# Two transfers for each late load, two subtractions written in pairs and two more zero products in an induced-set attention and mixture-of-experts kernel

## The chip, the cores and the metric

The kernel runs on one core of one Trainium2 chip. The metric is the time of one execution in device microseconds (us); lower is better. Every number below comes from three timed executions of the kernel before and from one more execution that was taken with the hardware profiler.

## What is computed

Four batches of 11456 rows of 128 numbers go through two attentions over 32 inducing points, and the result, seen as 45824 rows, through a soft mixture of experts (8 experts with 4 slots each, inner width 1024). The softmax over rows (`d`) runs down all 45824 rows, so no output can be finished before the last row has been read.

```python
def mab(q, kv):
    s = scale * (q @ kv.transpose(0, 2, 1))
    s = s - s.max(-1, keepdims=True)
    a = np.exp(s)
    a /= a.sum(-1, keepdims=True) + 1e-09
    return a @ kv
h = mab(I, x)
x = mab(x, h).reshape(B * S, D)
...
logits = x @ phi
d = np.exp(logits - logits.max(0, keepdims=True))
d /= d.sum(0, keepdims=True) + 1e-09
slot_input = d.T @ x
slot_out[e] = np.maximum(slot_input[e] @ w1[e], 0.0) @ w2[e]
...
c = np.exp(logits - logits.max(1, keepdims=True))
c /= c.sum(1, keepdims=True) + 1e-09
return c @ slot_out
```

All of it is in fp32.

## The kernel before

The rows are cut into 24 tiles, 6 for each batch; a tile n has 15 blocks of 128 rows, 1920 columns and 960 KB. A tile is read as rows (`xn`, n) and transposed (`xt`, n); for n from 6 on both lie ready in memory and are two loads, `ldn` (line 282) and `ldt` (line 294), each one transfer of 128 rows of 7680 bytes. The weights follow as nine loads `w` (lines 741 and 743). All loads, and later all stores of results (line 1020), are issued by SyncE (SP) in one fixed order. Each transfer carries one of eight completion semaphores in turn, and the issue of a transfer waits until the one that used its semaphore before, eight transfers earlier, has landed; some also wait until an engine has let go of the buffer.

Four stages follow each other, and overlap:

- First attention (L329 `s1p`, L340, L386, L389, L405 `ha`): scores of the inducing points against a tile, exponentials, and `ha`, 15 small products on a tile that add up over the six tiles of a batch. When the last tile of a batch is in, a short chain (hs, L461; htp, L464; hts, L467) gives the keys of the second attention.
- Second attention (L329 `s2p`, L576 and L579 on VectorE, then L583 on GpSimd, exponentials on ScalarE, L592 and L605 on TensorE, L635 on GpSimd): the logits of a tile go into `l_all`.
- Dispatch, by segments of three tiles: the maximum of the segment (`t`/`tm`, `pt`, `mc`, `pb`, `m_all`), then for each tile d = logits - maximum (L706, on GpSimd for 19 tiles and on VectorE for tiles 12, 20, 21, 22, 23), its exponential (L709) and the products `u` (L719). After the last segment `wl` (L814, GpSimd), `us_all` (L826 GpSimd, L842 VectorE) and `sit` (L845 to L852, TensorE) join the segments, VectorE copies them into `ma` (L863), and the experts run on TensorE: `hpm` (L872), `htm` (L885), `so` (L901), then `sos` and `sr` (L908, L911) give the slot outputs `srs`.
- Output: the softmax over slots of each tile (lines 511 to 547, 967, 970), four products `po` with `srs` (L1000), four copies out of PSUM (L1011, shared by ScalarE and VectorE) and the stores. Until `srs` is there no store can start.

A *fill* is a product of a zeroed 128x128 tile with itself into a free PSUM buffer (line 235, `warm_into`): nothing reads it. The kernel has ten: one early, one and six around tile 17 of the dispatch, and two before the experts.

The order of the work on every engine is written out by hand: `plan.order()` reads a string of numbers (`ORDER`), and each engine runs its operations in that order, strictly one after the other. What stands later on an engine waits, even if its own inputs are there.

Where a subtraction L706 writes its tile, `DW` lists the tiles that are written block after block: of each pair of blocks the 32 numbers of the one, then of the other, so that the write steps while the read runs straight. Tiles that are not listed are written as they are read, the two blocks of a pair interleaved, and `u` reads them with a step of two.

Of the kernel before, what the change touches and what calls it, by code (L numbers as in the profile page):

```python
# [26 lines left out]
WP = XW  # L27
NW = 2 * E * F // WP
# [5 lines left out]
HOST_T = [6, 7, 8, 9, 10, 11, 12, 13, 14, 15, 16, 17, 18, 19, 20, 21, 22, 23]  # L34
# [15 lines left out]
RINGS = {'x': 13, 's1': 6, 'e1': 2, 's2': 9, 'a2t': 2, 'd': 3, 'half': 1, 'cs': 3, 'mm': 8, 'h': 1, 'hts': 2, 'ht': 1, 'bdg': 2, 'hc': 4, 'bm': 6, 'bz': 8, 'cm': 6, 'cz': 6, 'tms': 2, 'xa': 1, 'xb': 1, 'xc': 1, 'xd': 1, 'xe': 1, 'xf': 1}  # L50
H = 1
HEAD = 1
NF = 10
ORDER = (
# [7 lines left out]
    "8h8u9Id2667H8t7J9J837L7O7MaNaz9B9K9C9W7P8g9L9Xaaabdi7K7N7Qb19Y9MaAaOaBb2aPb3btbubvbwbxbybzbAbCaCac9Z9NaDada0aQaRa1b4aEaFb5aeaf9O8va29P9R8waSb6a38xag9QaT8y8za49SahaGaiaHb7a6akaIbDaJ"  # L62
    "aUa5aj8A8D8Galb88BaV7RaK8EamaWaMb9baaXanao8HaYbbb0bE8C8Fi28Iapasbc8JbFbei3i4i5i6i7i8bfaqatavawbGbgar9DbhaubIbJbHbi9EbKaxbLbMbjbObmbpbkbnaLbdaZbPbBbqbQaybSbNbYbZdud3bRblbobrbVbTbUbW"
    "d4c0dcdDbXi9iac3c4dLd5dUe3dddjdndvdkebc5c7c8c9c1c6dodpdwdqcadrdldxdEcdcbceccdycfcgdzdFc2ekdAdGchdsdBdtesdHdIdCcicjfCfFfDfEfGfHfwdMdJfJfLdKfIdNfKfNfMfOfPgDdVdWfxfAfyfzfQdOdPgGgFgEgH"
    "e4dXfWfUdQfRfTfSdRg3e5g0fYfXg7dYdZfZg6g4dSdTece6e7edeeg5eBe0eJgxe8gzgygBefg9gagceggbgde1gAe2e9elgfeheReaeteiglgnejghgigjgmemeueveCgKgpggeneoeDgNewexepgMgrgOgsgugLgogvgWeqeygteZereE"
    "gXgQezeKeLeFgReAgYeGgTeMgSgUgZeNeOh0eHfBgIfVgJg2g1g8gegkgCgqgPh2h5heh6h3h4h1h7gVgweIf7ePeSf0hgh8hieTffeQeUf1hfhaf2f3eVf8hqfohbf4eWhshteXeYf5fgf9faf6fphuh9hrhhhchkhlfbfchCfhhmfdfihD"
    "hFfjfqhGhwfrfshyfefthEhvhjhdhAhzfkflhxfuhnfvhHhIhMhohJhKfmfnhLhOhVhZhNhWhPhShXhQhYhRi0hUhphBhT"
# [28 lines left out]
def tag_of(kind, a):  # L96
    return (XTAG if kind == "xt" else NTAG).get(a, "x")
# [51 lines left out]
def tile_kernel(ctx, tc, x0, xn, xt_d, ind_t, phi, w12, w3, consts, out):  # L149
    nc = tc.nc  # L150
# [121 lines left out]
    def load(a):  # L272
# [388 lines left out]
    def segment(k):  # L661
# [72 lines left out]
    def weights():  # L734
        for o in range(0, 2 * E * F, WP):
            m = min(WP, 2 * E * F - o)

            def ld(o=o, m=m):
                t = btile("x", ("w", o // WP))
                if m == WP:  # L740
                    nc.sync.dma_start(parts(t), w12[o // WP].rearrange("h p w -> p h w"))
                else:
                    nc.sync.dma_start(t[:, :m], w3)
                wt.append(t)

# [392 lines left out]
```

## Time and profile before

| what | value |
|---|---|
| median of 3 executions | 216.58 us (216.47 to 217.27) |
| the profiled execution | 217.6 us, of it 215.5 us span from the first to the last instruction |
| TensorE | busy 188.7 us (88%) |
| VectorE | busy 162.6 us (75%) |
| ScalarE | busy 135.5 us (63%) |
| GpSimd | busy 125.5 us (58%) |
| data moved | 73.87 MB, mean 343 GB/s |
| mean granted TensorE clock | 0.915 of full speed |

The page of the profile divides the span into 40 slices. By it TensorE is busy almost throughout, but a busy share is a mean over stages that wait for different things. The loads fill the transfer engines until about 126 us, the transfers then rest until about 155 us, and the stores fill them to the end. The granted clock is full until 140 us and falls to half in one slice there and again in parts of the last 45 us. To see what one stage waits for, read the order of time on one engine, with the idle time before an instruction and what ended it.

### The profile page before, as it was taken

How to read it: one execution, taken by the hardware profiler on the slowest of the kernel's cores; microseconds unless marked ns; L12 is line 12 of the kernel's file. 1: busy time of each engine (PE TensorE's matmuls, PEld its weight loads, DVE VectorE, ACT ScalarE, POOL GpSimd, SP SyncE). 2: the span in 40 equal slices, each digit the busy share in tenths (PEclk: the TensorE clock that was granted, in tenths of full speed). 3: DMA queues.
4: the chain of work that ended last, by engine and by line, in shares of the span. 5: the costliest groups of instructions: out<-in, count | busy, mean ns of one | idle time of the engine just before them, and what ended most of it. 6: DMA issues, size and time to landing. Idle time of an engine off the chain costs nothing.

```text
span 215.5 us, 6873 instructions
## 1 busy us (share of the span) xinstructions
PE 188.7 (88%) x2778; PEld 129.7 (60%) x2778; DVE 162.6 (75%) x375; ACT 135.5 (63%) x368; POOL 125.5 (58%) x138
## 2 busy tenths in 40 slices
PE   7699999999999999999798999899799998998100
PEld 7368574598465986559694688798454375342000
DVE  0114576999999999999598999995999789855400
ACT  2487541965856993269683988604599898963300
POOL 0000000549988489987876999996857867742000
PEclk9999999999999999999999999969999958755855
DMA  6999999998799999999999950000299999999994
GB/s 218 387 429 416 393 422 415 415 415 361 233 389 422 422 412 419 408 419 412 415 416 414 419 236 0 6 5 3 66 378 410 418 421 422 412 421 423 411 416 190
DMA packets 12799, 73.87 MB, mean 343 GB/s; under 512 B 1633, under 2 KB 2657, under 8 KB 12769
## 3 DMA queue, kind: packets, MB, share of 16 engines
q1 hardware_dynamic: 12336, 73.27, 84.1%
q8 instruction: 22, 0.36, 0.7%
q10 hardware_dynamic: 432, 0.17, 0.3%
q14 instruction: 9, 0.07, 0.1%
HBM read 49.84 MB, written 23.59 MB: 341 GB/s over the span
## 4 chain that ended last, share of the span: by engine, by line
PE 59%; DMA 10%; DVE 9%; POOL 7%; issue 4%; ACT 3%; SPq 1%; DVEq 0%; ACTq 0%; POOLq 0%
PE po L1000 10%; PE s1p L329 9%; PE ha L405 9%; PE s2p L329 7%; DMA w<-w 6%; PE lp L605 6%; DMA xn<-xn 4%; DVE ot L1011 4%; PE tt L592 4%; PE tp L306 3%; POOL d L706 3%; PE hpm L872 2%; POOL bt L583 2%; PE u L719 2%; DVE l_all L970 2%
## 5 line engine op out<-in xcount | busy, mean ns | idle before, releaser
L1000 PE MATMUL po<-l_all,srs 32*128 32x480 f32 (+1 forms) x200 | 43.6, 746 | 3.8 <-DVE l_all L970 1.8
L1000 PEld LDWEIGHTS po<-l_all,srs 32*128 32x128 f32 x200 | 22.0, 229 | 24.4 <-ACT ot L1011 10.5
L1011 ACT COPY ot<-po 128x480 f32<-128x480 f32 (+1 forms) x65 | 31.8, 576 | 7.4 <-PE po L1000 7.1
L583 POOL TENSOR_TENSOR bt<-bt,bm 128x480 f32<-128x480 f32 x24 | 23.6, 1001 | 16.6 <-DVE bm L579 14.1
L967 POOL TENSOR_TENSOR ct<-ct,cz 128x480 f32<-128x480 f32 x24 | 23.7, 996 | 9.2 <-DVE cz L547 9.2
L605 PE MATMUL lp<-bdg,a2t 128*128 128x132 f32 x192 | 25.7, 278 | 0.6 <-ACT d L709 0.6
L340 DVE TENSOR_SCALAR_CACHE_REDUCE s<-s1p 128x480 f32<-128x480 f32 (+1 forms) x24 | 15.0, 644 | 14.2 <-PE s1p L329 13.8
L635 POOL TENSOR_TENSOR bt<-bt,bz 128x480 f32<-128x480 f32 x24 | 23.5, 1003 | 2.8 <-DVE bz L617 1.9
L605 PEld LDWEIGHTS lp<-bdg,a2t 128*128 128x128 f32 x192 | 23.3, 190 | 1.8 <-ACT d L709 0.8
L1011 DVE COPY ot<-po 128x480 f32<-128x480 f32 (+1 forms) x35 | 20.2, 602 | 3.3 <-PE po L1000 3.3
L706 POOL TENSOR_TENSOR d<-l_all,m_all 128x512 f32<-128x512 f32 x19 | 21.8, 1173 | 1.3 <-ACT m_all L685 1.3
L520 POOL TENSOR_TENSOR ct<-l_all,cm 128x512 f32<-128x512 f32 x18 | 18.8, 1053 | 3.9 <-DVE l_all L970 2.4
L405 PE MATMUL ha<-xn,e 128*32 128x128 f32 x570 | 19.6, 275 | 1.6 <-issue 1.5
L329 PE MATMUL s1p<-xt,it_sb 128*32 128x480 f32 x160 | 19.8, 571 | 0.8 <-ACT xt L314 0.7
L386 ACT ACTIVATE s<-s,negm 128x480 f32<-128x480 f32 (+1 forms) x24 | 16.6, 697 | 5.7 <-DVE negm L371 5.7
L329 PE MATMUL s2p<-xt,hts 128*32 128x480 f32 x160 | 19.6, 571 | 0.0
L405 PEld LDWEIGHTS ha<-xn,e 128*32 128x32 f32 x570 | 16.5, 109 | 4.1 <-issue 2.2
L709 ACT ACTIVATE d<-d 128x512 f32<-128x512 f32 x24 | 14.9, 633 | 5.9 <-POOL d L706 5.0
L342 POOL MEMSET s<- 128x16 f32 x4 | 0.5, 117 | 31.1 <-DVE e L389 30.8
L970 DVE STREAM_TRANSPOSE l_all<-ct 128x480 f32<-128x480 f32 x24 | 15.8, 660 | 1.9 <-POOL ct L967 1.9
L389 DVE STREAM_TRANSPOSE e<-s 128x480 f32<-128x480 f32 x24 | 15.6, 657 | 1.9 <-ACT s L386 1.7
L576 DVE STREAM_TRANSPOSE bt<-s2p 128x480 f32<-128x480 f32 x24 | 15.6, 665 | 0.8 <-PE s2p L329 0.4
(136 smaller groups left out, 369.5 us busy)
## 6 DMA issues: line engine op xcount, KB each, us to landing
out<-ot SPq DMA_DIRECT2D x20, 960.0 KB, 8.0
xn<-xn SPq DMA_DIRECT2D x18, 960.0 KB, 13.1
xt<-xt SPq DMA_DIRECT2D x14, 960.0 KB, 13.9
w<-w SPq DMA_DIRECT2D x8, 960.0 KB, 14.4
l_all<-xn SPq DMA_DIRECT2D x5, 960.0 KB, 10.0
l_all<-xt SPq DMA_DIRECT2D x4, 960.0 KB, 6.4
out<-ot SPq DMA_DIRECT2D x6, 480.0 KB, 6.7
xn<-x SPq DMA_DIRECT2D x2, 256.0 KB, 3.3
```

Source lines behind the costliest of these rows:

```text
L329: nc.tensor.matmul(dst[32 * g : 32 * g + 32, :w], lhs, src, start=True, stop=True)
L386: nc.scalar.activation(t[:, :v], t[:, :v], AF.Exp, bias=T["negm", b, g], accum_out=z6[:, a : a + 1])
L405: nc.tensor.matmul(ha[32 * q : 32 * q + 32, :P], T["e1", a][:, j * S : (j + 1) * S], T["xn", a][:, j * P : (j + 1) * P], start=c == lo and ...
L520: nc.gpsimd.tensor_tensor(t.rearrange("p (a e s) -> p a e s", s=S, e=2), l_blocks(n), m, op=ALU.subtract)
L583: nc.gpsimd.tensor_tensor(t, t, T["bm", n][:, :nb].unsqueeze(2).broadcast_to(full), op=ALU.subtract)
L605: nc.tensor.matmul(pt[:, q * 4 * SZ : (q * 4 + m) * SZ], t[: m * S, q * P : (q + 1) * P], bdgs[b % 2].rearrange("p q s -> p (q s)")[: m * ...
L635: nc.gpsimd.tensor_tensor(t, t, T["bz", n][:, :nb].unsqueeze(2).broadcast_to(full), op=ALU.mult)
L706: e.tensor_tensor(t.rearrange(o, s=S, e=2), l_pairs(n), m, op=ALU.subtract)
L967: nc.gpsimd.tensor_tensor(t, t, T["cz", n][:, :nb].unsqueeze(2).broadcast_to([P, nb, S]), op=ALU.mult)
L970: nc.vector.transpose(l_of(n), T[ck][:, :w])
L1000: nc.tensor.matmul(ptile("mm", ("po", n, g, h))[:, : hi - lo], T["srs",][q, :], l_of(n)[q, lo:hi], start=True, stop=True)
L1011: (nc.vector.tensor_copy if dve else nc.scalar.copy)(T["ot", n][:, g * w + lo : g * w + hi], T["po", n, g, h][:, : hi - lo])
```

## The change

- `HS` names 20 loads (transposed tiles 18 to 23, row tiles 18 to 23, weights 0 to 7). Each becomes two transfers, columns 0 to 959 and 960 to 1919, into the same buffer, one issued right behind the other. In memory nothing moves; a row of a transfer is 3840 bytes instead of 7680. A product waits for the half that it reads.
- `DW` loses 20 and 22: the subtractions of these two tiles on VectorE write in pairs, as the read runs, and `u` reads with a step of two.
- `NF` goes from 10 to 12: two more fills, in the order at two places of the dispatch's end. The order of all else is the same; all numbers of the fills behind them move by one or two.

```diff
-DW = [3, 9, 14, 20, 22]
+DW = [3, 9, 14]
...
-H = 1
 HEAD = 1
-NF = 10
+HS = [('t', 18), ('t', 19), ('t', 20), ('t', 21), ('t', 22), ('t', 23), ('n', 18), ('n', 19), ('n', 20), ('n', 21), ('n', 22), ('n', 23), ('w', 0), ('w', 1), ('w', 2), ('w', 3), ('w', 4), ('w', 5), ('w', 6), ('w', 7)]
+NF = 12
...
-    "aUa5aj8A8D8Galb88BaV7RaK8EamaWaMb9baaXanao8HaYbbb0bE8C8Fi28Iapasbc8JbFbei3i4i5i6i7i8bfaqatavawbGbgar9DbhaubIbJbHbi9EbKaxbLbMbjbObmbpbkbnaLbdaZbPbBbqbQaybSbNbYbZdud3bRblbobrbVbTbUbW"
+    "aUa5aj8A8D8Galb88BaV7RaK8EamaWaMb9baaXanao8HaYbbb0bE8C8Fi2i38Iapasbc8JbFbei4i5i6i7i8i9bfaqatavawbGbgar9DbhaubIbJbHbi9EbKaxbLbMbjbObmbpbkbnaLbdaZbPbBbqbQaybSbNbYbZdud3bRbliabobrbVbT"
...
+        def halves(n):
+            w = XW // 2 if n in HS else XW
+            return [slice(o, o + w) for o in range(0, XW, w)]
+
         def ldn(lo, hi):
             def f():
                 t = T["xn", a] if ("xn", a) in T else xtile("xn", a)
                 if a:
-                    nc.sync.dma_start(parts(t), xn[a - 1].rearrange("h p w -> p h w"))
+                    for r in halves(("n", a)):
+                        nc.sync.dma_start(t[:, r], xn[a - 1][:, r])
...
             def ldt():
-                nc.sync.dma_start(parts(xtile("xt", a)), xt_d[HOST_T.index(a)].rearrange("h p w -> p h w"))
+                t = xtile("xt", a)
+                for r in halves(("t", a)):
+                    nc.sync.dma_start(t[:, r], xt_d[HOST_T.index(a)][:, r])
...
                 if m == WP:
-                    nc.sync.dma_start(parts(t), w12[o // WP].rearrange("h p w -> p h w"))
+                    for r in [slice(0, WP // 2), slice(WP // 2, WP)] if ("w", o // WP) in HS else [slice(0, WP)]:
+                        nc.sync.dma_start(t[:, r], w12[o // WP][:, r])
```

SP's queue in the last part of the loads, before (a name ends with a running number of its buffer; DMAHW are the eight completion semaphores, the number behind PE and DMAHW is part of their names):

```order
L294 DMA xt_22_1416<-xt 128x1920 [waits DMAHW7_49,PE_49]
L294 DMA xt_23_1418<-xt 128x1920 [waits DMAHW0_49,PE_49]
L282 DMA l_all_78<-xn 128x1920 [waits DMAHW1_49,PE_49]
L282 DMA xn_19_1421<-xn 128x1920 [waits DMAHW2_49]
L282 DMA xn_20_1423<-xn 128x1920 [waits DMAHW3_49]
```

and the first of the same loads after the change:

```order
L298 DMA xt_22_1420<-xt 128x960 [waits DMAHW3_49,PE_49]
L298 DMA xt_22_1420<-xt 128x960 [waits DMAHW4_49]
L298 DMA xt_23_1423<-xt 128x960 [waits DMAHW5_49,PE_49]
L298 DMA xt_23_1423<-xt 128x960 [waits DMAHW6_49]
L284 DMA l_all_78<-xn 128x960 [waits DMAHW7_49,PE_49]
L284 DMA l_all_78<-xn 128x960 [waits DMAHW0_49,PE_49]
```

Each load takes two semaphores of the eight, so at most eight halves are under way where it was eight wholes; the waits for buffers stand where they stood, on the first half.

TensorE around tile 17 of the dispatch, before (u_5 are the products of tiles 15 to 17, the part behind d_ and bt_ names the tile):

```order
L719 MATMUL u_5_2233<-d_16_2197,bt_16_1584 32x32 x15
L235 MATMUL fill_1_2264<-srs_83 128x128
L719 MATMUL u_5_2233<-d_17_2199,bt_17_1661 32x32 x15
L235 MATMUL fill_2_2289<-srs_83 128x128
L235 MATMUL fill_3_2291<-srs_83 128x128
```

and after:

```order
L723 MATMUL u_5_2253<-d_16_2217,bt_16_1597 32x32 x15
L232 MATMUL fill_1_2284<-srs_83 128x128
L232 MATMUL fill_2_2286<-srs_83 128x128
L723 MATMUL u_5_2253<-d_17_2219,bt_17_1674 32x32 x15
L232 MATMUL fill_3_2311<-srs_83 128x128
L232 MATMUL fill_4_2313<-srs_83 128x128
```

One fill more stands ahead of the products of tile 17; the six behind them are still six.

TensorE at the last segment, before (u_7 are the products of tiles 21 to 23, sit joins the segments):

```order
L719 MATMUL u_7_2406<-d_21_2376,bt_21_2068 32x32 x15
L719 MATMUL u_7_2406<-d_22_2380,bt_22_2070 32x32 x15
L719 MATMUL u_7_2406<-d_23_2382,bt_23_2074 32x32 x15
L845 MATMUL sit_2453<-sis_2404,cst_70 128x32
L849 MATMUL sit_2453<-us_all_82,h_3_2352 128x32
```

and after:

```order
L723 MATMUL u_7_2428<-d_21_2398,bt_21_2081 32x32 x15
L232 MATMUL fill_9_2444<-srs_83 128x128
L723 MATMUL u_7_2428<-d_22_2402,bt_22_2083 32x32 x15
L723 MATMUL u_7_2428<-d_23_2404,bt_23_2087 32x32 x15
L850 MATMUL sit_2477<-sis_2426,cst_70 128x32
L854 MATMUL sit_2477<-us_all_82,h_3_2374 128x32
```

One fill more stands between the products of tiles 21 and 22. Nothing else changes its place on any engine.

## Rows read from the trace of the kernel before

**Rows 1.** Busy time by stretch: start:end, length, each engine (instructions), clock, DMA share, GB/s.

```profile
core 0: us, PE busy (x) PEld busy (x) DVE busy (x) ACT busy (x) POOL busy (x), PEclk, DMA share, GB/s
104.00:117.00 13.00, 10.83 (x248) 8.77 (x236) 9.73 (x23) 7.39 (x25) 9.00 (x10) 1.00 1.02 416
117.00:132.00 15.00, 14.55 (x209) 10.88 (x210) 14.97 (x31) 12.66 (x40) 14.72 (x15) 1.00 0.68 277
132.00:142.00 10.00, 9.21 (x310) 7.91 (x309) 9.27 (x23) 6.11 (x19) 9.81 (x14) 0.97 0.01 3
...
158.00:202.00 44.00, 38.91 (x161) 19.43 (x158) 34.86 (x73) 35.98 (x82) 25.07 (x26) 0.77 1.02 417
```

**Rows 2.** TensorE in order of time: start, length, instructions [idle before <-what ended it].

```profile
106.63 0.30 PE L405 MATMUL ha<-xn,e 128*32 128x128 f32 x1 [1.53 <-issue]
...
108.98 1.84 PE L405 MATMUL ha<-xn,e 128*32 128x128 f32 x57
...
113.84 0.46 PE L605 MATMUL lp<-bdg,a2t 96*128 96x99 f32 x2 [0.65 <-ACT d L709]
```

**Rows 3.** Busy time between these stalls; DMA queues from 104.2 to 105.5 us.

```profile
106.62:113.83 7.21, 6.56 (x125) 6.02 (x125) 6.51 (x14) 4.85 (x17) 5.03 (x6) 1.00 1.01 415
...
q8 instruction: 1, 0.02, 5.3%
```

**Rows 4.** Line 282 from 89.1 to 89.5 us: the load of row tile 23.

```profile
L282 SPq DMA_DIRECT2D xn<-xn x1: 328/328/328, 89.3 to 89.3; - x1
...
DMA to landing us min/median/max: 20.2/20.2/20.2
```

**Rows 5.** GpSimd in order of time, from the first tile of the last batch.

```profile
116.94 1.00 POOL L583 TENSOR_TENSOR bt<-bt,bm 128x480 f32<-128x480 f32 x1 [0.90 <-DMA w<-w]
...
139.02 1.32 POOL L764 MEMSET ma<- 128x1440 f32 x1
140.45 0.25 POOL L826 TENSOR_TENSOR us_all<-us_all,wl 128x32 f32<-128x32 f32 x1
```

**Rows 6.** VectorE in order of time: subtractions of tiles 12 and 20, and the experts.

```profile
117.24 0.68 DVE L706 TENSOR_TENSOR d<-l_all,pb 128x512 f32<-128x512 f32 x1
...
134.69 1.09 DVE L706 TENSOR_TENSOR d<-l_all,pb 128x512 f32<-128x512 f32 x1
...
147.01 0.29 DVE L890 COPY ma<-htm 128x128 f32<-128x128 f32 x1 [1.68 <-PE htm L885]
```

**Rows 7.** TensorE in order of time at the end of the dispatch.

```profile
132.62 0.49 PE L235 MATMUL fill<-srs 128*128 128x128 f32 x2
133.24 0.45 PE L719 MATMUL u<-d,bt 128*32 128x32 f32 x30
...
139.68 0.89 PE L719 MATMUL u<-d,bt 128*32 128x32 f32 x60 [0.65 <-ACT d L709]
...
141.22 0.95 PE L235 MATMUL fill<-srs 128*128 128x128 f32 x4
142.10 4.61 PE L872 MATMUL hpm<-w,ma 128*32 128x128 f32 x112
```

**Rows 8.** Line 872 (hpm) alone, in two stretches; columns TensorE, weight loads, clock, DMA.

```profile
142.10:144.90 2.80, 2.80 (x56) 2.60 (x59) 0.50 0.03 9
144.92:146.70 1.78, 1.78 (x64) 1.52 (x56) 1.00 0.00 0
```

**Rows 9.** The output stage: stores issued from 160.1 to 164 us, busy stretches, TensorE.

```profile
out<-ot SPq DMA_DIRECT2D x3, 480.0 KB, 7.0
...
165.50:169.50 4.00, 4.00 (x21) 1.89 (x20) 2.47 (x6) 4.00 (x11) 3.91 (x4) 1.00 1.02 412
175.00:179.00 4.00, 4.00 (x22) 3.26 (x18) 3.32 (x8) 3.55 (x9) 1.51 (x3) 0.50 1.01 417
...
155.79 6.32 PE L1000 MATMUL po<-l_all,srs 32*128 32x480 f32 x38 [0.23 <-DVE l_all L970]
...
193.13 2.52 PE L1000 MATMUL po<-l_all,srs 32*128 32x480 f32 x8 [0.47 <-DVE cz L547]
```

More of the change, by code (lines that the diff above doesn't have):

```diff
@@ L62 @@
     "8h8u9Id2667H8t7J9J837L7O7MaNaz9B9K9C9W7P8g9L9Xaaabdi7K7N7Qb19Y9MaAaOaBb2aPb3btbubvbwbxbybzbAbCaCac9Z9NaDada0aQaRa1b4aEaFb5aeaf9O8va29P9R8waSb6a38xag9QaT8y8za49SahaGaiaHb7a6akaIbDaJ"
-    "aUa5aj8A8D8Galb88BaV7RaK8EamaWaMb9baaXanao8HaYbbb0bE8C8Fi28Iapasbc8JbFbei3i4i5i6i7i8bfaqatavawbGbgar9DbhaubIbJbHbi9EbKaxbLbMbjbObmbpbkbnaLbdaZbPbBbqbQaybSbNbYbZdud3bRblbobrbVbTbUbW"
[L64 to L67, printed above, removed]
+    "aUa5aj8A8D8Galb88BaV7RaK8EamaWaMb9baaXanao8HaYbbb0bE8C8Fi2i38Iapasbc8JbFbei4i5i6i7i8i9bfaqatavawbGbgar9DbhaubIbJbHbi9EbKaxbLbMbjbObmbpbkbnaLbdaZbPbBbqbQaybSbNbYbZdud3bRbliabobrbVbT"
+    "bUbWd4c0dcdDbXibicc3c4dLd5dUe3dddjdndvdkebc5c7c8c9c1c6dodpdwdqcadrdldxdEcdcbceccdycfcgdzdFc2ekdAdGchdsdBdtesdHdIdCcicjfCfFfDfEfGfHfwdMdJfJfLdKfIdNfKfNfMfOfPgDdVdWfxfAfyfzfQdOdPgGgF"
+    "gEgHe4dXfWfUdQfRfTfSdRg3e5g0fYfXg7dYdZfZg6g4dSdTece6e7edeeg5eBe0eJgxe8gzgygBefg9gagceggbgde1gAe2e9elgfeheReaeteiglgnejghgigjgmemeueveCgKgpggeneoeDgNewexepgMgrgOgsgugLgogvgWeqeygteZ"
+    "ereEgXgQezeKeLeFgReAgYeGgTeMgSgUgZeNeOh0eHfBgIfVgJg2g1g8gegkgCgqgPh2h5heh6h3h4h1h7gVgweIf7ePeSf0hgh8hieTffeQeUf1hfhaf2f3eVf8hqfohbf4eWhshteXeYf5fgf9faf6fphuh9hrhhhchkhlfbfchCfhhmfd"
+    "fihDhFfjfqhGhwfrfshyfefthEhvhjhdhAhzfkflhxfuhnfvhHhIhMhohJhKfmfnhLhOhVhZhNhWhPhShXhQhYhRi0hUhphBhT"
 )
 SHAPES = {
-    "x0": (P, XW), "xn": (NT - 1, H, P, XW // H), "xt": (len(HOST_T), H, C, XW // H), "ind_t": (C, S), "phi": (C, S),
-    "w12": (NW, H, P, XW // H), "w3": (P, 2 * E * F - NW * WP), "consts": (P, 2 * P + 5),
+    "x0": (P, XW), "xn": (NT - 1, P, XW), "xt": (len(HOST_T), C, XW), "ind_t": (C, S), "phi": (C, S),
+    "w12": (NW, P, XW), "w3": (P, 2 * E * F - NW * WP), "consts": (P, 2 * P + 5),
 }
@@ L189, in xtile @@
         return T[kind, a]
-    def parts(t):
-        return t.rearrange("p (h w) -> p h w", h=H)
     def blocks(t):
@@ L1094 @@
             xt[HOST_T.index(a), :, : nb * P] = part.transpose(3, 0, 2, 1).reshape(C, nb * P)
-    def cut(t):
-        return np.ascontiguousarray(t.reshape(-1, P, H, XW // H).transpose(0, 2, 1, 3))
     w1 = inputs["moe_w1"].transpose(1, 0, 2)
@@ L1107 @@
         "x0": xn[0],
-        "xn": cut(xn[1:]),
-        "xt": cut(xt),
+        "xn": np.ascontiguousarray(xn[1:]),
+        "xt": xt,
         "ind_t": np.ascontiguousarray(inputs["inducing"].T),
         "phi": np.ascontiguousarray(inputs["moe_phi"]),
-        "w12": cut(w12[:, : NW * WP].reshape(P, NW, WP).transpose(1, 0, 2)),
+        "w12": np.ascontiguousarray(w12[:, : NW * WP].reshape(P, NW, WP).transpose(1, 0, 2)),
         "w3": np.ascontiguousarray(w12[:, NW * WP :]),
```

## The prediction

> **What bounds the kernel now.** I read busy time by stretch first, to see who is full where; then each engine in order of time, for the idle time before an instruction and what ended it; then the output stage. Up to 126 us the loads fill the transfer engines: from 104 to 117 us they move 416 GB/s. Yet TensorE, VectorE, ScalarE and GpSimd all idle in part there, with 10.83, 9.73, 7.39 and 9.00 us busy of 13. From 117 to 132 GpSimd is busy for 14.72 of 15 us, from 132 to 142 for 9.81 of 10 [rows 1]. So the end of the dispatch is GpSimd's chain, and what comes before it decides when that chain starts.
>
> TensorE in order of time shows two stalls in the first stretch: 1.53 us ahead of 106.63 and 0.65 us ahead of 113.84 [rows 2]. The first is put down to "issue": the trace shows nothing that it waits for. The second is put down to ScalarE's `d`, which I doubt, because of the count between them: 125 products and 125 weight loads, 250 instructions, and a few that are not counted as busy. During the first stall there is also one packet of the queue of instructions, 0.02 MB, 5.3% of 16 engines in 1.3 us, that is one engine for 1.1 us [rows 3]. My reading is that TensorE ran out of instructions both times and waited for the next block of its program, which came through transfer engines that were full of loads.
> By the Trainium skill (Runtime: NRT & Kernel Launch, "Instruction fetch mechanics") instructions arrive in blocks of 256 and the crossing is "mostly hidden". The count between the stalls agrees with the block; the two stalls, 1.53 and 0.65 us, are not hidden.
>
> How far can the first stretch move? The load of row tile 23 is issued at 89.3 and lands 20.2 us later, at 109.5 [rows 4]. The products `ha` of tile 23 are the last of the 57 that run from 108.98 to 110.82 [rows 2]. They can't start before 109.5, whatever the stall ahead did. Behind them hs, htp and hts lead to GpSimd's first `bt` of the last batch at 116.94, which had waited 0.90 us. From there GpSimd runs almost without a break to the memset of `ma` (139.02 to 140.34) and `us_all` at 140.45 [rows 5]. Then sit, `ma`, hpm, htm, so and srs follow in a chain, the first `po` runs at 155.79, and the stores take 417 GB/s from 158 us on [rows 1, 9]. The amount to store is fixed, so the end is the first store plus a constant, while tiles come fast enough.
>
> **The change, part by part: the halved loads.** They add 20 transfers. An issue on SP takes 0.33 us [rows 4]. A half of 480 KB at 416 GB/s takes 1.18 us, so SP keeps ahead and the issues cost nothing; if that cover were gone, 20 issues would cost 6.6 us. The rate of transfers that large can be read in the output stage, whose first stores are of 480 KB: 412 GB/s while halves land, 417 later with wholes [rows 9]. That is 1.2% of the 12 halved tiles ahead of tile 23's end, 12 x 0.983 MB at 417 GB/s or 28 us: +0.35 us on the landing at 109.5, and I bound it by 0 and 0.7. The extra waits fall on halves that land before the other half, so they delay no product beyond what the whole did.
> The Trainium skill (DMA: Bandwidth & Descriptors, "Rules for kernel authors") speaks against this part: it asks for at least 1 MiB for each transfer. By its figure the halves would lose rate; the row of 412 against 417 GB/s says that with eight queued they lose about 1%.
>
> What may be gained is the two stalls. At most eight halves are queued instead of eight wholes, and rows of a transfer are half as long, so an instruction block has less ahead of it. Bounds: 0 (the wait doesn't depend on what is queued) and 1.53 + 0.65 = 2.2 us. The first stall can't give its whole 1.53: without it the 57 products could run from about 107.5, but tile 23 still lands at 109.5. Its 15 products, 15/57 of 1.84 = 0.5 us, would then end at 110.0 instead of 110.82: 0.8 us, less the 0.35 that the rate takes from the landing, 0.45. The second stall stands behind that, on the way to GpSimd's `bt`: 0.65 us. I take 0.45 + 0.65 = 1.1 us, the sum of what the two caps leave; what is late next is tile 23's landing. GpSimd waited for 0.90 us at 116.94 [rows 5] and follows TensorE there; any gain beyond 0.9 needs its earlier work to move too, which also runs behind TensorE's stalls.
>
> **Two subtractions in pairs.** Tile 12, not in `DW`, takes 0.68 us on VectorE; tile 20, in it, takes 1.09 [rows 6]. So VectorE saves 0.41 us twice. The cover is GpSimd, busy to 139.02 and on to 140.34 with the memset that stands ahead of `us_all` [rows 5]: 0 on the path. Without that cover it would be worth up to 0.65 us, TensorE's wait for a `d` at 139.68 [rows 7]. `u` read with a step of two is not slower where it can be seen: 30 products take 0.45 us for 15 of either kind, and the 60 at the end take 0.89 [rows 7].
>
> **Two fills.** Two fills take 0.49 us and four 0.95, so one costs 0.24 [rows 7]. The first new one goes where TensorE has 0.13 us free (133.11 to 133.24), so tile 17's products come 0.1 us later; the segment's maximum behind them is used after GpSimd's own queue, so nothing on the path. The second goes into the 0.65 us gap ahead of 139.68 and costs nothing there; if `d` comes earlier by then, up to 0.24.
>
> What a fill may bring is the clock. It is 0.97 on the mean from 132 to 142 [rows 1] and half from 142.10 to 144.90, just after the stretch with the 0.65 us gap. In that time 56 products of hpm take 2.80 us, 50.0 ns each; at the full clock 64 take 1.78, 27.8 ns each [rows 8]. So the dip costs 56 x 22.2 = 1.24 us on hpm. The four fills ahead of it take 0.95 us from 141.22 [rows 7]; two of them were at half clock, and I estimate that they hold hpm up by 0.3 us. VectorE's copy waits 1.68 us for htm [rows 6], so 1.55 us can go before something else is late. Bounds: 0 (the dip stays, or moves a little) and 1.55. The gap filled is the one idle stretch that I see close ahead of the fall, so I lean to the dip going; no row shows that 0.24 us of fill is enough.
>
> **The sum** against the profiled execution: 217.6 - 1.1 (stalls) - 1.55 (clock) - 0 (pairs, fills) = 214.95 us. That execution is 1.0 us above the median of 216.58, and nothing tells whether the timed ones paid the whole dip. I count half of the clock term there: 216.58 - 1.1 - 0.8 = 214.7 us.
>
> **The rivals.**
> B, only the clock: the instruction blocks come as late as before, because what is queued does not set their wait. For it: I infer the mechanism from one packet and one count. 216.58 - 0.8 = 215.8 us.
> C, only the stalls: the dip stays or moves into another part of hpm. For it: the fill closes a third of one gap only, and TensorE was busy for 9.21 of 10 us anyway [rows 1]. 216.58 - 1.1 = 215.5 us.
> D, it does not do what it says: neither the stalls nor the dip go, or the rate of the halves (up to +0.7 us at tile 23) eats what is gained. 216.6 us, up to 217.3.
> E, slower: the stores run dry. From 158 to 202 us the clock is 0.77 [rows 1]. At the full clock 38 `po` take 6.32 us, 1.33 for the eight of one tile; at half the eight take 2.52 us [rows 9], and the 960 KB of a tile's stores at 417 GB/s take 2.36. So at half clock TensorE alone is slower than the stores, at the full one far faster. If the new timing moves the clock's falls so that some 7 us more of the output stage run at half, three tiles take 2.52 instead of 1.33 us, 3.6 us in all; the lead that the stores still have there, which I put at about 1.6 us, comes off, and the last store goes 2 us later: 218.6 us without the gains. It decides from the point at which the last `po` is delayed by more than the first store is advanced. Against it: VectorE and ScalarE have idle time to give, and the transfers are still full up to 202 us [rows 1].
>
> **How the numbers follow.** A, both as summed: 214.7 us, chance 0.37, its own range 213.9 (the whole clock term) to 215.6 (half of both terms). B 0.18, C 0.20, D 0.13, E 0.12. A measurement of this kernel can tell some 0.5% from no change: below 215.5 is faster, above 217.66 slower. Faster: nearly all of A (0.35), a third of B (0.07) and half of C (0.10), 0.52. Slower: E, 0.12. The rest, 0.36, is the same. The range leaves out E and the far ends of A and D, under 2 in 10: 213.5 to 217.0 us.
>
> **What would show it.** Right: no gap of TensorE over 0.4 us near 105 and 113 us, GpSimd's `bt` at about 115.8 instead of 116.94, the gap ahead of 139.68 partly filled by a fill, hpm's 120 products in about 3.3 us instead of 4.6 at a granted clock of 1.00, the subtractions of tiles 20 and 22 at 0.68 us, the first `po` at about 153 and 415 GB/s or more to the end. Wrong: the stalls at the same length with half the queue (the fetch reading falls, B); hpm still with products of 50 ns (C); halved loads that land later than 109.5 by over 0.7 us (D); transfer shares under 1 before the last store (E).

## The result, and the profile after

The changed kernel takes 214.85 us (median of 5, 214.65 to 215.45); the kernel before, run beside it, 217.27 (median of 5, 216.47 to 217.50). The ratio is 0.9891, with a 95% interval of 0.9857 to 0.9926: faster by 0.7 to 1.4%. Forecast were 214.7 us and faster. In a second comparison (e0 below) the ratio was 0.9931 (0.9900 to 0.9961). The profiled execution took 214.67 us with a span of 212.2; before it was 217.6 with 215.5.

Busy time by stretch shows first where the time went. The columns are those of [rows 1].

```profile
104.00:117.00 13.00, 12.52 (x281) 9.62 (x277) 11.75 (x27) 8.42 (x30) 10.56 (x12) 1.00 1.03 405
117.00:132.00 15.00, 14.58 (x274) 11.58 (x265) 14.93 (x32) 13.35 (x42) 15.00 (x16) 1.00 0.82 322
130.00:140.00 10.00, 9.83 (x315) 8.46 (x315) 8.87 (x24) 6.79 (x20) 9.92 (x15) 1.00 0.02 5
158.00:202.00 44.00, 35.62 (x143) 17.49 (x140) 32.31 (x67) 32.70 (x75) 24.07 (x25) 0.75 1.02 417
```

From 104 to 117 us TensorE is busy for 12.52 us where it was 10.83, and every other engine gains with it; the loads move 405 GB/s there instead of 416. GpSimd's stretch behind it is as full as it was. The output stage moves the same 417 GB/s, at a granted clock of 0.75 on the mean (before 0.77).

TensorE in order of time (start, length, instructions, in brackets the idle time before and what ended it), the places of [rows 2] and [rows 7]. A product stands in these rows as two records: the 15 products `u` of one tile are x30, and the x60 of `ha` are two tiles. Where products are counted below, it is these records.

```profile
103.81 1.97 PE L409 MATMUL ha<-xn,e 128*32 128x128 f32 x60
...
107.83 1.52 PE L409 MATMUL ha<-xn,e 128*32 128x128 f32 x44
109.83 0.65 PE L409 MATMUL ha<-xn,e 128*32 128x128 f32 x16 [0.48 <-DMA xn<-xn]
...
111.91 1.04 PE L609 MATMUL lp<-bdg,a2t 128*128 128x132 f32 x8
...
112.99 1.01 PE L333 MATMUL s2p<-xt,hts 128*32 128x480 f32 x8
...
137.60 0.49 PE L232 MATMUL fill<-srs 128*128 128x128 f32 x2
138.01 0.85 PE L723 MATMUL u<-d,bt 128*32 128x32 f32 x60
...
139.69 0.69 PE L232 MATMUL fill<-srs 128*128 128x128 f32 x4
140.31 3.26 PE L877 MATMUL hpm<-w,ma 128*32 128x128 f32 x112
```

The 60 products `ha` that broke at the 1.53 us stall run through, and so do the eight `lp` that broke at the 0.65 us stall. What is late next is what the prediction named: tile 23's load, for whose second half `ha` waits 0.48 us. The fill stands in the gap ahead of the last `u`, and 112 products of hpm take 3.26 us instead of 4.61.

GpSimd, the places of [rows 5], and VectorE, those of [rows 6]:

```profile
115.58 1.00 POOL L587 TENSOR_TENSOR bt<-bt,bm 128x480 f32<-128x480 f32 x1 [0.86 <-DVE bm L583]
...
137.66 1.30 POOL L769 MEMSET ma<- 128x1440 f32 x1
138.92 0.25 POOL L831 TENSOR_TENSOR us_all<-us_all,wl 128x32 f32<-128x32 f32 x1
...
133.30 0.68 DVE L710 TENSOR_TENSOR d<-l_all,pb 128x512 f32<-128x512 f32 x1
```

An account in raw times, before minus after: `bt` 116.94 - 115.58 = 1.36 us; `us_all` 140.45 - 138.92 = 1.53; hpm's start 142.10 - 140.31 = 1.79; the 38 products `po` of [rows 9] 155.79 against 152.65 = 3.14. Behind that nothing more is gained but 0.2 to 0.3 us. So of the 3.3 us of span between the two profiled executions 1.4 us arise at the stalls, 0.2 in the dispatch, and 1.6 between `us_all` and the end of hpm, where the clock had fallen before.

### The profile page after: what moved, and what is told of

Read it like the earlier page. It is cut to its first block, busy times and chain, and to the rows that moved or that the text cites. A ratio compares the mean times of both kernels' runs of the same rounds, so it can differ in the third digit from the quotient of the medians.

```text
span 212.2 us, 6908 instructions
## 1 busy us (share of the span) xinstructions
PE 188.3 (89%) x2782; PEld 129.6 (61%) x2782; DVE 162.1 (76%) x375; ACT 135.2 (64%) x368; POOL 125.2 (59%) x138
## 4 chain that ended last, share of the span: by engine, by line
PE 43%; DMA 27%; DVE 10%; POOL 4%; issue 3%; ACT 3%; SPq 3%; DVEq 0%; POOLq 0%; ACTq 0%
DMA xn<-xn 23%; PE po L1005 10%; PE ha L409 5%; PE s1p L333 5%; DMA xt<-xt 5%; DVE ot L1016 4%; PE s2p L333 4%; PE lp L609 4%; PE tp L310 3%; DVE l_all L975 2%; POOL bt L587 2%; SPq L284 2%; PE hpm L877 2%; PE so L906 2%; PE u L723 2%
## 5 line engine op out<-in xcount | busy, mean ns | idle before, releaser
L1005 PEld LDWEIGHTS po<-l_all,srs 32*128 32x128 f32 x200 | 21.9, 222 | 24.3 <-ACT ot L1016 12.2
L333 PE MATMUL s1p<-xt,it_sb 128*32 128x480 f32 x160 | 20.4, 571 | 0.7 <-ACT xt L318 0.7
L975 DVE STREAM_TRANSPOSE l_all<-ct 128x480 f32<-128x480 f32 x24 | 15.8, 661 | 1.9 <-POOL ct L972 1.8
```

Of the source, the lines that this page charges most:

```text
L333: nc.tensor.matmul(dst[32 * g : 32 * g + 32, :w], lhs, src, start=True, stop=True)
L975: nc.vector.transpose(l_of(n), T[ck][:, :w])
L1005: nc.tensor.matmul(ptile("mm", ("po", n, g, h))[:, : hi - lo], T["srs",][q, :], l_of(n)[q, lo:hi], start=True, stop=True)
```

## A common point to count from

The executions differ in their first 80 us, which the change doesn't touch: the load of row tile 17, the last ahead of the halved ones, lands anywhere between 79.6 and 83.3 us. (In e1, the latest of the table, the granted clock is 0.79 over the first 16 us, where it is 1.00 in before and after; what makes the others differ was not followed.) A timed median carries this scatter, so I read the traces from that landing on. The table is worked out from the traces, one execution each: us after the landing of tile 17. "hpm" is the time from the start of its first product to the end of its last. The first stall is the one ahead of `ha`, the second the one in `lp`; 0 is no idle time over 0.2 us there.

| kernel | what is halved; pairs; fills | 1st stall | 2nd stall | tile 23 lands | bt | us_all | hpm | ratio to before (95%) |
|---|---|---|---|---|---|---|---|---|
| before | none; no; 10 | 1.53 | 0.65 | 29.64 | 37.12 | 60.63 | 5.56 | 1 |
| after | t, n, w; yes; 12 | 0 | 0 | 29.62 | 35.42 | 58.76 | 4.21 | 0.9891 (0.9857 to 0.9926) |
| e0 | the same again | 0 | 0.34 | 29.48 | 35.89 | 59.22 | 4.22 | 0.9931 (0.9900 to 0.9961) |
| e1 | t, n, w; no; 10 | 0 | 0 | 29.70 | 35.50 | 58.97 | 4.22 | 0.9980 (0.9943 to 1.0016) |
| e2 | none; yes; 12 | 1.27 | 0.51 | 28.52 | 37.13 | 60.46 | 4.22 | 0.9992 (0.9956 to 1.0027) |
| e3 | t, n, w; yes; 10 | 0 | 0.55 | 29.64 | 36.26 | 59.58 | 4.22 | 0.9950 (0.9918 to 0.9981) |
| e4 | t, n, w; no; 12 | 0 | 0.63 | 29.06 | 35.76 | 59.25 | 4.22 | 0.9918 (0.9883 to 0.9952) |
| e5 | n, w; yes; 12 | 1.52 | 0.51 | 29.75 | 36.97 | 60.30 | 4.22 | 0.9987 (0.9952 to 1.0022) |
| e7 | w; yes; 12 | 0.92 | 0.28 | 28.96 | 36.41 | 59.73 | 4.21 | 0.9962 (0.9927 to 0.9997) |
| e8 | t; yes; 12 | 0 | 0.22 | 28.56 | 35.33 | 58.63 | 4.21 | 0.9906 (0.9868 to 0.9944) |
| e9 | t, w; yes; 12 | 0 | 0 | 29.50 | 36.00 | 59.32 | 4.21 | 0.9900 (0.9861 to 0.9938) |
| e11 | t; no; 10 | 0 | 0.22 | 28.98 | 35.75 | 59.24 | 4.21 | 0.9986 (0.9938 to 1.0033) |

(t are the transposed tiles 18 to 23, n the row tiles, w the weights; e0 to e4, e5 and e7 ran on one chip, e8 and e9 on a second, e11 on a third; e1 to e4 were one comparison, e0, e5 and e7 another. e6 and e10 stand in the text alone.)

## Experiments

### One part at a time

e1, the halves alone: the list of halves stays, the rest as before. (The order string goes back to that of before together with `NF`, here and in e3 and e11.)

```diff
-DW = [3, 9, 14]
+DW = [3, 9, 14, 20, 22]
...
-NF = 12
+NF = 10
...
```

> Only the halved loads; ten fills and the five written tiles as before. My theory (the two stalls of TensorE are waits for instruction blocks behind full transfer queues, and halves shorten them; the clock is the fills' doing): no gap of TensorE over 0.5 us put down to issue between 100 and 118 us, GpSimd's first bt of the last batch at 115.6 +- 0.3, hpm still with a stretch at half clock (its 112 products about 4.5 us), time 215.5 to 216.0. Rival 1 (the stalls went for another reason than the halves): both stalls back at about 1.5 and 0.65 us, time as before, 216.6 to 217.3. Rival 2 (the dip went because TensorE no longer stalls, not by the fills): hpm's 112 products in 3.3 us and time 214.7 to 215.2.

Measured: no stall, and `bt` at 35.50 from tile 17's landing, as my theory had it. (In raw time it stands at 118.76, outside the 115.3 to 115.9 expected, because this execution was 3.1 us behind that of after when tile 17 landed.) But hpm ran at the full clock, with ten fills, where I had it at half. TensorE at the end of the dispatch of e1:

```profile
141.47 0.88 PE L723 MATMUL u<-d,bt 128*32 128x32 f32 x60 [0.64 <-ACT d L713]
...
143.00 0.69 PE L232 MATMUL fill<-srs 128*128 128x128 f32 x4
143.62 3.26 PE L877 MATMUL hpm<-w,ma 128*32 128x128 f32 x112
```

The gap ahead of the last `u` is 0.64 us, as in the kernel before, and no dip follows it. So that gap doesn't decide by itself, and in this execution no new fill was needed. The median was 216.06 us against 216.87 for before, with a ratio that includes 1.

e2, all but the halves:

```diff
-HS = [('t', 18), ('t', 19), ...]
+HS = []
```

> All of the change but the halved loads. My theory: the two stalls come back (some 1.5 and 0.65 us near 105 and 113 us), bt at about 116.9, hpm at the full clock, 3.3 us; time 214.85 + 1.36 = 216.2, between 215.7 and 216.6. Rival 1 (halves do nothing): 214.85. Rival 2 (clock by the stalls): hpm at half clock again, 216.6 to 217.3.

Measured: 216.27 us, as expected, and both stalls are back at their places:

```profile
104.67 1.94 PE L409 MATMUL ha<-xn,e 128*32 128x128 f32 x59
107.88 0.30 PE L409 MATMUL ha<-xn,e 128*32 128x128 f32 x1 [1.27 <-issue]
...
114.95 0.47 PE L609 MATMUL lp<-bdg,a2t 96*128 96x99 f32 x2 [0.51 <-ACT d L713]
```

`bt` stands at 37.13 against 35.42 with halves: the halves are worth 1.7 us at that point. By these traces it is the halves that take the stalls away.

e3, all but the two new fills (`NF` and the order of before), and e4, all but the pairs (`DW` of before):

```diff
 (e3)
-NF = 12
+NF = 10
...
 (e4)
-DW = [3, 9, 14]
+DW = [3, 9, 14, 20, 22]
```

> All of the change but the two new fills. My theory: no stalls at 105 and 113 us, the stretch at half clock back in hpm (112 products about 4.5 us), time 214.85 + 1.3 = 216.2, between 215.6 and 216.5. Rival (the fills are not what keeps the clock): hpm in 3.3 us, 214.85 within 0.4.

> All of the change, but tiles 20 and 22 written block after block again. My theory (VectorE's 0.41 us twice lie beside GpSimd's work): 214.85 within 0.3, us_all at 138.9 as with pairs. Rival (with GpSimd earlier by 1.4 us, VectorE has become the late one and the pairs are worth up to 0.65 us): 215.2 to 215.5, TensorE waiting for d ahead of its last products u.

e3 ran hpm at the full clock too, in 3.26 us: the rival. But it doesn't repeat the gap of before as e1 does, because the pairs have shortened it to 0.24 us:

```profile
139.86 0.96 PE L723 MATMUL u<-d,bt 128*32 128x32 f32 x60 [0.24 <-ACT d L713]
```

Its time, 215.33 us and 0.9950, lies between. e4 cost nothing that can be measured in time (0.9918 against 0.9931 for e0). Its 215.35 us and a wait of 0.22 us for `d` ahead of the last `u` are what its rival forecast, but the changed kernel itself took 215.34 us on that chip (e0), so the time doesn't speak for the rival. In the trace the pairs show as 0.16 us: from `bt` to `us_all` it takes 23.51 us in before, 23.47 to 23.49 in e1, e4 and e11, which have no pairs, and 23.32 to 23.34 in after, e0, e2 and e3, which have them. In both e3 and e4 the second stall is there (0.55 and 0.63 us) in spite of the halves, and in after and e1 it is not. Of the eight kernels of the table with halved transposed tiles five show it, at 0.22 to 0.63 us; of the four with whole ones all do, at 0.28 to 0.65. So halves make it rarer, they don't rule it out.

### Which halves

e0 is the changed kernel once more, beside e5, e6 and e7 on one chip.

> The changed kernel itself, beside the next three on one chip. Its first stall (of 1.3 to 1.5 us in the kernels with wholes) stays away; the second, which was there at 0.55 and 0.63 us in two of the four traces with halves and absent in two, may or may not show. GpSimd's first bt of the last batch 35.4 to 36.3 us after the landing of the last whole load ahead of the halves (before and with wholes 37.1). Time 0.6 to 1.2% under before. If the dip of the clock in hpm were the fills' doing it never shows here; if it falls by chance, as the two traces with ten fills and no dip suggest, it can show here too.

It gave 215.34 us, no first stall and no dip, but 0.34 us of the second stall, ahead of the same two `lp` as before:

```profile
112.82 0.46 PE L609 MATMUL lp<-bdg,a2t 96*128 96x99 f32 x2 [0.34 <-ACT d L713]
```

e5 halves the row tiles and weights only, e7 the weights only:

```diff
 (e5)
-HS = [('t', 18), ..., ('n', 18), ..., ('w', 0), ...]
+HS = [('n', 18), ..., ('w', 0), ...]
 (e7)
+HS = [('w', 0), ...]
```

> Halves for the row tiles 18 to 23 and the weights, the transposed tiles whole. My theory (halves cost 2% of the loads' rate, and only what is queued at the two stalls matters): the stalls as in the changed kernel, tile 23 lands about 0.5 us earlier against the last loads before the halves (6 tiles fewer at 0.09 us), bt up to 0.4 us earlier; time 0 to 0.4 us under the changed kernel of the same chip. Rival (the transposed halves bring something, since half a tile can be worked on earlier): 0.2 to 0.5 us over it.

> Only the weights in halves, tiles whole. My theory (a stall is set by what is queued when TensorE crosses into its block): the first stall, when the queue holds row tiles, is there at 1.2 to 1.5 us; the second, when it holds weights and the last row tiles, is gone or under 0.4; bt 36.2 to 36.6 us after the last whole load before; time 0.3 to 0.8 us over the changed kernel. Rival (any halving shifts things by chance): no such order, first stall absent or both there.

e5 went against my theory and its rival: not a little faster or slower, the whole first stall was back, and 216.61 us.

```profile
104.64 1.94 PE L409 MATMUL ha<-xn,e 128*32 128x128 f32 x59
108.10 0.30 PE L409 MATMUL ha<-xn,e 128*32 128x128 f32 x1 [1.52 <-issue]
...
115.17 0.46 PE L609 MATMUL lp<-bdg,a2t 96*128 96x99 f32 x2 [0.51 <-ACT d L713]
```

Its last whole transposed tile lands at 95.4 us; when TensorE stalls at 106.6, the queue has held nothing but halves for 11 us. So what is queued at the stall is not what decides. e7 kept a first stall of 0.92 us (1.2 to 1.5 were expected) and shortened the second to 0.28; 215.71 us.

e8 is the complement of e5, only the transposed tiles in halves; e9 has these and the weights.

```diff
 (e8)
+HS = [('t', 18), ('t', 19), ('t', 20), ('t', 21), ('t', 22), ('t', 23)]
 (e9)
+HS = [('t', 18), ..., ('t', 23), ('w', 0), ..., ('w', 7)]
```

> Only the six transposed tiles in halves, row tiles and weights whole: the complement of e5. Told apart: the first stall came with every kernel whose transposed tiles are whole (packet of instructions near 91 us asked for, 6.8 to 7.0 us late) and with none whose transposed tiles are halves. If the block that is late is the one that is asked for while the transposed tiles are queued, the first stall is gone here (its packet 15.4 to 15.8 us after the last whole load before, against 17.9), tile 23 lands 0.4 to 0.6 us earlier than with 20 halves, and bt stands 35.4 to 36.3 us after that landing: time as the changed kernel within 0.5 us. Rival (halved rows are needed too, because the next block is asked for among them): a first stall of 0.8 us or more, time 0.8 to 1.5 us over the changed kernel.

> Transposed tiles and weights in halves, only the row tiles whole. First theory of e8: first stall gone, second as with weights in halves (absent or under 0.6 us), time as the changed kernel or up to 0.5 us under it, since the row tiles land at the rate of wholes. Rival of e8: first stall of 0.8 us or more and 0.5 to 1.5 us over it.

e8: 214.78 us against 217.05, no first stall, and what is left of the second is 0.22 us. TensorE of e8:

```profile
104.61 1.95 PE L409 MATMUL ha<-xn,e 128*32 128x128 f32 x60
...
113.19 0.46 PE L609 MATMUL lp<-bdg,a2t 96*128 96x99 f32 x2 [0.22 <-issue]
```

e9: 214.59 us. So in these two six of the 20 halved loads, the transposed ones, carry what the halves bring. The queue of instructions tells more. A packet of it is 16 KB and occupies one engine for 1.0 to 1.1 us; below are the stretches of 1.2 or 1.3 us that hold one whole packet each, first of e2 (99.0 to 100.2 and 105.3 to 106.5 us), then of e8 (95.6 to 96.8 and 103.0 to 104.3). The columns are packets, MB and the share of 16 engines.

```profile
q8 instruction: 1, 0.02, 5.3%
...
q8 instruction: 1, 0.02, 5.3%
```

```profile
q8 instruction: 1, 0.02, 5.3%
...
q8 instruction: 1, 0.02, 4.9%
```

Counted from tile 17's landing, the first of these packets comes at 18.2 us in e2 and 14.7 in e8; in all kernels with whole transposed tiles (before, e2, e5, e7) at 17.9 to 18.2, in all with halved ones (after, e0, e1, e3, e4, e8, e9) at 14.7 to 15.8, in e11 at 17.0. The next one follows 6.0 to 6.5 us later in the former and 6.2 to 7.7 later in the latter. So a late packet comes already one block before the stall's own. That fits a block asked for while transposed tiles are queued, of which the last lands 14.1 to 15.2 us behind tile 17; when a block is asked for, no trace shows. It is not TensorE that moved. Counted in products and weight loads, it reaches its 2945th instruction, 250 ahead of the first stall, 20.4 to 21.4 us behind tile 17 in all twelve kernels of the table. The stall's own packet starts 3.35 to 4.04 us after that where the packet before was late, and 1.35 to 1.80 us after it where it was not (2.29 in e11). e11 only just got through: that packet ends at 24.3 us, and TensorE reaches the block at 25.5. How a late packet delays the next one, and why e5's second doesn't catch up, although it waits among halves, these runs don't say.

e6 has the same 20 loads cut by partitions:

```diff
-            w = XW // 2 if n in HS else XW
-            return [slice(o, o + w) for o in range(0, XW, w)]
+            w = P // 2 if n in HS else P
+            return [slice(o, o + w) for o in range(0, P, w)]
...
-                        nc.sync.dma_start(t[:, r], xn[a - 1][:, r])
+                        nc.sync.dma_start(t[r], xn[a - 1][r])
...
```

> The same 20 loads in two transfers each, but cut by partitions: 64 rows of 7680 bytes instead of 128 of 3840. It tells the bytes that are queued from the length of a row. Theory 1 (what counts is how many bytes stand ahead of an instruction block, eight halves instead of eight wholes): first stall gone as with halves by column, its packet about 22.4 us after the last whole load's landing, against 24.4 with wholes; rate 413 GB/s or more if short rows are what cost it; time as the changed kernel within 0.4. Theory 2 (shorter rows let the block in): the stall of 1.3 to 1.5 us is back, time 0.8 to 1.2 us over the changed kernel.

It took 247.37 us (median of 6; the profiled execution 254.69) and can't answer what it was made for, since the rate fell. Busy time by stretch in e6, the last column GB/s:

```profile
70.00:110.00 40.00, 29.85 (x461) 19.56 (x463) 25.53 (x59) 17.23 (x53) 22.64 (x24) 0.83 1.03 260
110.00:150.00 40.00, 28.38 (x497) 21.11 (x487) 23.71 (x54) 18.55 (x60) 19.32 (x21) 0.91 1.03 236
```

The transfer engines are full (1.03) at 236 to 260 GB/s. Whether the bytes ahead of a block or the length of its neighbours' rows count was not settled.

### Is it the instructions?

e10 is e2 with 64 instructions more at the very start of TensorE:

```diff
-        warm_into(ptile("mm", ("warm0",)), 8)
+        wt = ptile("mm", ("warm0",))
+        warm_into(wt, 4)
+        for _ in range(20):
+            nc.tensor.matmul(wt[:1, :1], wz[:, :1], wz[:, :1], start=True, stop=True)
```

> The kernel with wholes of e2 with 16 tiny products more in the warm-up of TensorE at the start (20 of one column and 4 full ones for 8 full ones), 64 instructions more ahead of all else; loads and work as in e2. If the stalls are waits for blocks of TensorE's program, they stay at the same number of instruction (about the 3195th and the 3445th of TensorE's products and weight loads) and so stand 64 instructions earlier in the work: the first no longer ahead of the first product ha of a tile but among the products ahead of it, the second likewise earlier in lp or ahead of it. Rival (the stalled products wait for something that the trace doesn't show): the stall stays ahead of the same product ha, then the 3259th.

It ran once, in 218.83 us, so its time says nothing; the trace is what it was made for. Measured: no stall ahead of `ha` or in `lp`. The two stalls of that stretch stand elsewhere:

```profile
100.88 0.75 PE L596 MATMUL tt<-cst,bt 128*96 128x128 f32 x5 [0.67 <-issue]
...
107.56 1.95 PE L409 MATMUL ha<-xn,e 128*32 128x128 f32 x60
...
121.73 1.80 PE L333 MATMUL s2p<-xt,hts 128*32 128x480 f32 x10 [0.90 <-issue]
```

Busy time up to the first stall and from there to the second, in e2 and then in e10; what matters are the counts of PE and PEld:

```profile
0.00:107.87 107.87, 102.68 (x1597) 73.07 (x1597) 81.12 (x199) 68.12 (x191) 55.60 (x63) 1.00 0.97 390
107.87:114.94 7.07, 6.56 (x125) 6.03 (x125) 6.38 (x14) 4.84 (x17) 5.13 (x6) 1.00 1.02 415
```

```profile
0.00:100.87 100.87, 97.36 (x1472) 67.45 (x1472) 73.22 (x181) 59.21 (x163) 47.93 (x55) 1.00 0.94 376
100.87:120.83 19.96, 19.81 (x377) 15.91 (x377) 18.22 (x42) 15.39 (x51) 15.78 (x16) 1.00 1.02 415
```

In e2 TensorE stalls after 2 x 1597 = 3194 instructions and after 250 more, 3444; before, e5 and e7 have 1597 ahead of their first stall too. In e10 it stalls after 2944 and after 3698, which is 250 below the one and 254 above the other. All four numbers lie on one grid of 250 to 254, though the work moved by 64 instructions against it. A wait of one product for an unseen event would have moved with the product, to 3258. My expectation had the stalls at the very same numbers and missed that: which line of the grid stalls changed, the grid didn't. The packets agree. In all 15 stalls, the 13 of the table and the two of e10, the stalled product starts 1.2 to 1.5 us after the end of a packet of q8, whether the profile puts the wait down to "issue" or to ScalarE's `d`. That the stalls are waits for blocks of TensorE's program I take as shown.

### The smallest edit

e11 is the kernel before with the six transposed tiles in halves and nothing else.

```diff
 DW = [3, 9, 14, 20, 22]
...
+HS = [('t', 18), ('t', 19), ('t', 20), ('t', 21), ('t', 22), ('t', 23)]
 NF = 10
...
```

> The kernel before with one edit: the six transposed tiles 18 to 23 in halves; row tiles and weights whole, ten fills, five written tiles. If this edit carries the whole gain: no first stall, GpSimd's first bt 35.3 to 36.3 us after the landing of the last whole load ahead of tile 18's (before 37.1), us_all 23.5 us behind it (23.3 with the pairs), time 0.6 to 1.1% under before, at most 0.2 us over the kernel with transposed halves, pairs and twelve fills. If the fills matter, hpm shows the stretch at half clock here (5.6 us from its first product to its last instead of 4.2) and the time is 0.8 us or more above that kernel's, 0.2 to 0.5% under before.

Its trace does what was expected: no first stall, `bt` at 35.75, `us_all` 23.49 behind it. Of the second stall 0.22 us are left. The timed executions don't confirm it: 0.9986, with an interval from 0.9938 to 1.0033. TensorE in e11 again has the gap and the full clock:

```profile
112.34 0.46 PE L609 MATMUL lp<-bdg,a2t 96*128 96x99 f32 x2 [0.22 <-issue]
...
138.16 0.89 PE L723 MATMUL u<-d,bt 128*32 128x32 f32 x60 [0.66 <-ACT d L713]
...
139.70 0.69 PE L232 MATMUL fill<-srs 128*128 128x128 f32 x4
140.32 3.26 PE L877 MATMUL hpm<-w,ma 128*32 128x128 f32 x112
```

## What stays open: the clock

Of the traces with ten fills (before, e1, e3, e11) one shows the stretch at half clock in hpm, of those with twelve (after, e0, e2, e4, e5, e7, e8, e9, e10) none. That fits the fills, and it fits chance: three of four without them did without the dip, two of these (e1 and e11) with the gap of before ahead of the last `u`. (e6, which has twelve fills too, is slowed throughout and no match for the others: its granted clock is 0.85 from 178 to 190 us, and its 112 products of hpm take 4.32 us.)

The times point both ways. The kernels with halved transposed tiles and twelve fills stand at 0.9891 to 0.9931, those with ten at 0.9950 to 0.9986; the middle values, 0.9906 and 0.9980, differ by 0.7%, 1.6 us, and a dip costs 1.61 us (5.56 - 4.21 = 1.35 in hpm, 0.26 ahead of it). That would be the fills' doing if most executions without them had the dip. But e2 and e5, with twelve fills and pairs and no dip in their traces, stand at 0.9992 and 0.9987, and would have to be as far under the kernel before. A timed execution gives a span and a mean clock, and the mean is made by the output stage: in after it is 0.925, so 2 x 0.075 x 212 = 32 us are at half clock, none of them in hpm. So the dip can't be read in them directly.

The traces allow an estimate. Counted from tile 17's landing, the span of before ends at 135.71 us, without the dip's 1.61 at 134.10; after ends at 132.00, e2 at 133.60, e5 at 133.58, e8 at 131.89. Taken over 217 us, and with no dip in any timed execution, such ends give 0.990 for after and e8 and 0.998 for e2 and e5, and of the eleven measured intervals of the table ten hold their own value; e1 alone is off (0.992, where 0.9943 to 1.0016 was measured). With the dip in every timed execution of before and in none with twelve fills, after and e8 would stand at 0.982 to 0.983 and e2 and e5 at 0.990, outside all four intervals. So the timed executions of before seldom paid the dip, by this estimate from one trace of each kernel. How often it falls with and without the fills is not settled.

None of these kernels is shown to be faster than the changed one. e8, with 6 halved loads instead of 20, is as fast as far as these runs tell.

## Why the prediction was right, and where it only came out right

**The stalls, 1.1 us: right in kind, the size above it.** `bt` moved by 1.36 us in raw time and by 1.70 from tile 17's landing (after), 1.23 (e0), 1.62 (e1). The first stall was worth 0.8 us (the end of the last `ha` at 30.31 against 31.11) where I had 0.45; the second 0.9 at the start of `s2p` where I had 0.65. The cap was the one named: with the stall gone `ha` waits for tile 23's landing.

One reading behind the 0.45 was wrong, and that it did little harm is luck. The 15 products of tile 23 are 30 of the records, not 15 of the 57, and take 0.97 us instead of 0.5. Behind a tile that lands whole they would have ended at 110.5 instead of 110.82, and the 0.35 us of the rate would have taken what was gained. What made up for it is the halved row tile, in which only 16 records wait for the second half: `ha` ends 0.69 us behind tile 23's landing in after, and 1.21 us in e9, whose row tiles are whole:

```profile
109.36 0.96 PE L409 MATMUL ha<-xn,e 128*32 128x128 f32 x27 [0.34 <-DMA xn<-xn]
```

**What halving does: the wrong place.** I took it that a block waits behind what is queued when TensorE stalls. e5 and e8 show that it is the transposed tiles that take the first stall away: with the rows and weights halved it stayed at 1.52 us. The step of the prediction that failed is "an instruction block has less ahead of it", read for the packet in the stall; the lateness begins one block earlier.

**The rate, +0.35 us within 0 to 0.7: about right.** From 80 to 110 us the rows below give 403 to 404 GB/s in after and 414 to 415 in e2, 2.6% less, where I took 1.2% from the stores. On tile 23's landing the six kernels with halved row tiles have 29.5 us in the mean, the six with whole ones 29.0, with a scatter of half a microsecond in each.

```profile
80.00:95.00 15.00, 14.96 (x300) 8.51 (x296) 14.54 (x33) 7.18 (x20) 14.74 (x16) 1.00 1.03 404
95.00:110.00 15.00, 14.52 (x303) 12.79 (x299) 14.06 (x38) 12.63 (x39) 12.23 (x14) 1.00 1.03 403
...
80.00:95.00 15.00, 14.31 (x289) 7.74 (x278) 13.88 (x31) 7.20 (x20) 14.75 (x16) 1.00 1.02 414
95.00:110.00 15.00, 13.31 (x256) 11.69 (x253) 12.37 (x34) 10.56 (x34) 10.13 (x12) 1.00 1.02 415
```

The first two rows are of after, the last two of e2. The rule of the Trainium skill that the prediction weighed (DMA: Bandwidth & Descriptors, "Rules for kernel authors", at least 1 MiB for each transfer) points the right way, and the price is these 2.6%.

**The pairs, 0: nearly.** 0.68 instead of 1.09 us for tile 20, and 0.16 us of it arrives at `us_all`. The cover by GpSimd was thinner by that than I read.

**The clock, 1.55 us in the profiled execution, 0.8 on the median: not shown.** Between the two profiled executions 1.61 us went there, as the sum had it (142.10 - 140.45 + 5.56 = 7.21 before, 140.31 - 138.92 + 4.21 = 5.60 after). That the two fills brought it isn't shown, since three executions with ten fills went without the dip, and by the estimate above the timed executions of before seldom paid it. Then the 0.8 us in the forecast came from a trace of before that happened to hold a dip, and the forecast came out right by luck: the stalls gave 0.1 to 0.6 us more than I took for them (e0 and after) and the pairs 0.16. Of the 2.42 us between the two medians measured side by side these leave 0.6 to 1.0 without a cause; of the 1.5 us of e0's ratio they leave next to nothing. (Two counts were records as well: hpm's 120 products are 112, of which eight straddle the two stretches of [rows 8], and "two fills" in 0.49 us are one, "four" in 0.95 two. Neither changes the sum.)

**The slower rival, E.** Its condition, some 7 us more of the output stage at half clock, did not come. From 158 to 202 us the granted clock is 0.75 on the mean, 0.77 before, which is 1 to 2 us more at half. What changed is the place of the falls:

```profile
170.00:180.00 10.00, 9.11 (x45) 6.21 (x42) 9.42 (x19) 9.02 (x21) 6.77 (x7) 0.83 1.02 419
180.00:190.00 10.00, 9.53 (x30) 4.38 (x28) 6.95 (x16) 7.80 (x20) 5.64 (x7) 0.52 1.01 416
...
170.00:180.00 10.00, 9.85 (x42) 6.94 (x43) 9.32 (x21) 8.90 (x21) 6.57 (x8) 0.66 1.01 418
180.00:190.00 10.00, 9.29 (x34) 3.80 (x32) 7.72 (x16) 8.31 (x19) 8.15 (x9) 0.79 1.01 418
```

The first two rows are of after, the last two of before. In after the stores kept 416 to 419 GB/s from 170 to 202 us, so no price fell due. What 7 us more at half would cost, no run shows.

## What to carry to other kernels

A gap of TensorE put down to "issue" in a long unrolled kernel whose transfer queues are full can be a wait for the next block of its program: count instructions from one such gap to the next, and from the start, in two versions of the kernel. If the counts agree while the work differs, look at the loads that were queued one block earlier, not only at those in flight at the stall. Here cutting six loads in two took the first stall away in every trace, though alone (e11) it was not measured to be faster. And before a gain is put down to an edit, look whether the cost it removes is there in every execution: one profile can't tell a cost from a chance.

## What the runs showed of the hardware that was not expected

- Cutting a load by partitions (64 rows of 7680 bytes) took the rate from 415 to 236 to 260 GB/s with the transfer engines full. The Trainium skill (DMA: Bandwidth & Descriptors, "The descriptor swizzle") says of a transfer to 128 partitions that partitions 0 to 63 are written through the even ports and 64 to 127 through the odd ones. No run here shows the ports; e6 shows that 0.57 to 0.63 of the rate was left.
- A late block of instructions was followed by a late one: in e5 the next packet came 6.3 us after the late one, as in e2, though the queue held halves by then, and TensorE stood still for 1.52 us.
- After the end of a block's packet the stalled product started 1.2 to 1.5 us later, in 15 stalls of ten traces.
